# First two tiles of a fused attention and GELU kernel: 64x64 score products on plain transposed k, casts and loads in a new order

## The chip, the cores and the metric

The kernel runs on one core of a Trainium2 chip. The metric is the device time of one execution in microseconds, as a median over runs. A profile of one execution shows what each engine did: TensorE (PE, with its weight loads as PEld), VectorE (DVE), ScalarE (ACT), GpSimd (POOL), and SyncE (SP), whose queue issues the DMAs.

## The reference

```
q, k, v: (8, 8, 576, 64) fp32      w_in: (512, 2048)   w_out: (2048, 512)

for each batch b, head h and chunk of 64 rows (9 chunks of 576):
    scores = q_c @ k_c.T / 8
    attn   = exp(scores - max) / sum(exp(scores - max))
    out    = attn @ v_c
x = out as (8 * 576, 8 * 64) = (4608, 512)
h = x @ w_in
y = (0.5 * h * (1 + erf(h / sqrt 2))) @ w_out          # (4608, 512) fp32
```

Each chunk of 64 rows attends only to itself, so the attention is small: 64x64 scores for each of 576 pairs of head and chunk. The two dense products hold nearly all of the arithmetic.

## The kernel before

**Tiles.** The work is cut into nine tiles of 512 tokens: tile t < 8 holds eight chunks of batch t, the last tile the ninth chunk of all batches. Each tile goes through attention, which fills `x`, then through `mm1_slot` (16 slices f of 128 hidden columns, four matmuls of 128x512 each over ks, Gelu on ACT into `h`) and `mm2_slot` (four blocks of 128 tokens, 16 matmuls each). The attention of tile t+1 is put, by hand, between the matmuls of tile t. The order of instructions on every engine is the order in which the program writes them (`tc.manual_schedule`).

**Groups.** Two heads make a group g, four groups a tile. Of each group, q and k arrive in fp32 (`load_qk`), are cast to bf16 (`cast_qk`), transposed by TensorE into PSUM (`transposed`, four matmuls of 128x128) and copied back to SBUF: q into `qT` (`att_Tq`, L181), k into `k_bd` (`att_Tk`, L188). `k_bd` is block-diagonal: its off-diagonal blocks are zeroed once (`zero_k`), and the two heads are copied into the diagonal ones, so that one 128x128 product per chunk gives both heads' scores (`att_S`, L296, eight matmuls of 64 columns). ACT takes the exponential into `pT`.

**Sums.** The sum of the exponentials over keys runs along partitions. In tile 0, groups 0 and 1 use a product with `ones_bd` and two DVE transposes around a reciprocal (`att_sum`), groups 2 and 3 products with `ones_r` and back with `ident_f` (`att_sum_pe`, L348 and L357) and an ACT copy (L361). Tile 1 uses `att_sums` and `att_rc`. `att_av` multiplies with the block-diagonal `v_bd`, which `cast_v` (L169) fills, four quarter casts a group, and DVE scales the result into `x` (L372).

**Tiles 2 to 8** take another road: DMA transposes and 64x64 products on four quadrants of the array (`quad_S`, L227, and `quad_av`, L279). The change doesn't touch them.

**The opening.** All loads go through SP's queue, in program order, into six staging buffers used in turn: q and k of tile 0 in four parts each, v in eight, w_in in pieces of 512 columns, then w_out in four pieces (`load_w_out`) with q, k and v of tile 1 between them. Every piece is cast to bf16 by DVE, ACT or POOL as the program says. `keep_warm` issues matmuls on zeros whose result nobody reads.

**Tile 0's dense part.** `mm1_slices` computes the first two slices of h (L405), `phase` the rest (L415) and then the second product. For tile 0 that goes by rows of f (`mm2_rows`, L488, slots 0 to 11: every token block at once, so that w_out may arrive late), then by token blocks (L434, slots 12 to 15). The dictionary handed to `phase` says which parts of tile 1's attention stand ahead of which slot; `T`, `S_`, `U` and `A` are its lists of transposes, scores, sums and AV products. PSUM is shared out in three pools: `ps_mm` (three buffers), `ps_tp` (two, the transposes, and tile 1's later scores and AV), `ps_at` (three).

Of the kernel before, what the change touches and what calls it, by code (L numbers as in the profile page):

```python
# [11 lines left out]
def kernel(  # L12
# [9 lines left out]
    nc = tc.nc  # L22
# [45 lines left out]
    v_bds = [consts.tile([P, CT, G, P], bf16, name=f"v_bd{i}") for i in range(NV)]  # L68
    k_bds = [consts.tile([P, CT, P], bf16, name=f"k_bd{i}") for i in range(G)]

    def zero_v(i, eng):
        eng.memset(v_bds[i][0:CH, :, :, CH:P], 0.0)
        eng.memset(v_bds[i][CH:P, :, :, 0:CH], 0.0)

    def zero_k(k_bd, eng):
        eng.memset(k_bd[0:CH, :, CH:P], 0.0)
        eng.memset(k_bd[CH:P, :, 0:CH], 0.0)

# [98 lines left out]

    def att_Tq(t, g, copy):
        tp = transposed(t, "q", g)
        qT = work.tile([P, CT, CH], bf16, tag="qT", name="qT", bufs=5)  # L180
        copy(qT[:].rearrange("p i (c j) -> p i c j", j=J), tp)  # L181
        tiles[t]["qT", g] = qT

    def att_Tk(t, g, copy):
        tp = transposed(t, "k", g)
        for r in range(2):
            sl = slice(CH * r, CH * (r + 1))
            copy(k_bds[g][sl, :, sl].rearrange("p i (c j) -> p i c j", j=J), tp[sl])  # L188


# [100 lines left out]
    def att_S(t, g):  # L291
        st = tiles[t]
        pool, tag = (ps_tp, "tp") if t == 1 and g > 1 else (ps_at, "at")
        s_ps = pool.tile([P, CT, CH], f32, tag=tag, name="s_ps")
        for i in range(CT):
            nc.tensor.matmul(s_ps[:, i, :], k_bds[g][:, i, :], st["qT", g][:, i], start=True, stop=True)  # L296
        pT = work.tile([P, CT, CH], bf16, tag="pT", name="pT", bufs=5)
        nc.scalar.activation(pT[:], s_ps[:], Act.Exp, scale=scale)
        st["pT", g] = pT

    def att_sum(t, g, later=False):
        pT = tiles[t]["pT", g]
        sum_ps = ps_at.tile([P, MT], f32, tag="at", name="sum_ps")
        nc.tensor.matmul(sum_ps[:], ones_bd[:], pT[:], start=True, stop=True)
        t1 = work.tile([P, NB, 32], f32, tag="t1", name="t1", bufs=2)
        rc = work.tile([P, NB, 32], f32, tag="rc", name="rc", bufs=4)
        tiles[t]["rc", g] = rc
        nc.vector.transpose(t1[:], sum_ps[:].rearrange("p (n e) -> p n e", e=32))

        def rest_of_it():  # L310
            r1 = work.tile([P, NB], f32, tag="r1", name="r1", bufs=2)
            nc.vector.reciprocal(r1[:], t1[:, :, 0])
            nc.vector.transpose(rc[:], r1[:].to_broadcast([P, NB, 32]))
        if later:
            return rest_of_it
        rest_of_it()

# [46 lines left out]

    def att_av(t, g):
        st = tiles[t]
        pool, tag = (ps_tp, "tp") if t == 1 and g > 1 else (ps_at, "at")
        av_ps = pool.tile([P, CT, CH], f32, tag=tag, name="av_ps")
        for i in range(CT):
            nc.tensor.matmul(av_ps[:, i, :], v_bds[t % NV][:, i, g, :], st["pT", g][:, i, :], start=True, stop=True)  # L370
        x, av, rc = st["x"][:, g, :], av_ps[:].rearrange("p i e -> p (i e)"), st["rc", g][:]
        nc.vector.tensor_tensor(x, av, rc.rearrange("p n e -> p (n e)"), op=mybir.AluOpType.mult)  # L372

    NB = MT // 32
    DV, AC, PO = nc.vector.tensor_copy, nc.scalar.copy, nc.gpsimd.tensor_copy

    def att_units(t, cq=DV, ck=DV):
        tiles[t]["x"] = xpool.tile([P, G, MT], bf16, tag="x", name="x")
        T = []
        for g in range(G):  # L380
            T += [lambda g=g: att_Tq(t, g, cq), lambda g=g: att_Tk(t, g, ck if t == 0 or g % 2 == 0 else DV)]
        S_ = [lambda g=g: att_S(t, g) for g in range(G)]
        if t > 0:
            U = [lambda g=g: att_rc(t, g) for g in range(G)]
        else:
            U = [lambda g=g: att_sum(t, g) for g in range(G)]
        A = [lambda g=g: att_av(t, g) for g in range(G)]
        return T, S_, U, A


# [19 lines left out]
    def mm1_slot(t, f):  # L410
        if f == 0:
            tiles[t]["h"] = hpool.tile([P, FF, MT], bf16, tag="h", name="h")
        h_ps = ps_mm.tile([P, MT], f32, tag="mm", name="h_ps")
        for ks in range(KS):
            nc.tensor.matmul(h_ps[:], w_in_sb[:, ks, f * P:(f + 1) * P], tiles[t]["x"][:, ks, :],  # L415
                             start=(ks == 0), stop=(ks == KS - 1))
        nc.scalar.activation(tiles[t]["h"][:, f, :], h_ps[:], Act.Gelu)  # L417

    NQ = 4
# [92 lines left out]

    NWC = 4
    WC = d_ff // NWC
    FC = FF // NWC

# [9 lines left out]

    def load_w_out(c):
        raw = stage_tile()[:].rearrange("p (f n) -> p f n", f=FC)
        nc.sync.dma_start(raw, w_out_v[:, c * FC:(c + 1) * FC, :])

        def cast(i, copy):
            copy(w_out_sb[:, c * FC + i, :], raw[:, i, :])
        return cast

    def keep_warm(n):
        warm = ps_mm.tile([P, MT], f32, tag="mm", name="warm")
        for _ in range(n):
            nc.tensor.matmul(warm[:], rest[:, 0:P], rest[:], start=True, stop=True)

# [5 lines left out]
    with tc.manual_schedule():  # L545
# [5 lines left out]
        act_table(Act.Exp)  # L551
        keep_warm(7)
        zero_k(k_bds[0], nc.gpsimd)
        zero_k(k_bds[1], nc.gpsimd)
        zero_v(0, nc.vector)
        T, S_, U, A = att_units(0, DV, AC)
        cast_qk(0, "k", 0, PO)
        zero_k(k_bds[2], nc.gpsimd)
        cast_qk(0, "k", 1, PO)
        zero_k(k_bds[3], nc.gpsimd)  # L560
        cast_qk(0, "k", 2, PO)
        cast_qk(0, "k", 3, PO)
        for g in range(G - 1):
            for r in range(2):
                cast_v(0, g, r, (PO, PO))
        cast_v(0, G - 1, 0, (PO, PO))
        win[0](0, PO)
        cast_qk(0, "q", 0, DV)
        T[0]()
        cast_qk(0, "q", 1, DV)  # L570
        T[1]()
        keep_warm(3)
        T[2]()
        S_[0]()
        T[3]()
        cast_qk(0, "q", 2, DV)
        keep_warm(1)
        T[4]()
        keep_warm(1)
        S_[1]()  # L580
        cast_qk(0, "q", 3, DV)
        U[0]()
        T[5]()
        T[6]()
        T[7]()
        U[1]()
        S_[2]()
        keep_warm(1)
        S_[3]()
        keep_warm(1)  # L590
        act_table(Act.Gelu)
        p2 = att_sum_pe(0, 2)
        p3 = att_sum_pe(0, 3)
        A[0]()
        A[1]()
        p2()
        cast_v(0, G - 1, 1, (DV, DV))
        A[2]()
        win[0](1, AC)
        p3()  # L600
        A[3]()
        win.append(load_w_in(NWC - 1))
# [3 lines left out]
        load_qk(1, "q")  # L606
        wout.append(load_w_out(1))
        for c in range(1, NWC):
            for i in range(4):
                win[c](i, DV if i % 2 == 0 else PO)  # L610
            if c == 1:
                load_qk(1, "k")
            else:
                wout.append(load_w_out(c))
            if c < 3:
                r = slice(CH * (c - 1), CH * c)
                o = slice(CH * (2 - c), CH * (3 - c))
                nc.gpsimd.memset(v_bds[1][r, :, :, o], 0.0)
# [3 lines left out]
        for g in range(G):  # L622
            cast_qk(1, "q", g, DV if g == 0 else PO)
        for i in range(FC):
            wout[1](i, DV if i % 2 == 0 else PO)
        for g in range(G):
            cast_qk(1, "k", g, DV if g % 2 == 0 else PO)
        for i in range(FC):
            wout[2](i, PO)
# [5 lines left out]

        T, S_, U, A = att_units(1, AC, AC)
        def next_qk():
            for nm in "qk":
                load_qk(2, nm)
        over = []  # L640

        def sums():
            over.append(att_sums(1))
            over[0](1)
        mm, at = (ps_mm, "mm"), (ps_at, "at")
        mm1_slices(0, (mm, mm), (((0, 1), range(KS)),))
        phase(0, {0: [lambda: act_table(Act.Exp)],
                      2: [T[0]], 3: [T[2]], 4: [T[4], T[6]], 7: [T[1], T[3]], 8: [T[5], S_[0]],
                      9: [T[7], S_[1], next_qk], 10: [S_[2], lambda: att_sum(1, 0), lambda: wout[3](2, DV)],
                      11: [lambda: wout[3](3, AC), S_[3]], 12: [lambda: cast_v(1, 1, 0, (AC, AC)), lambda: cast_v(1, 1, 1, (AC, AC)), sums],  # L650
                      13: [A[0], lambda: over[0](2), lambda: over[0](3), U[1]], 14: [A[1], U[2]], 15: [A[2], U[3]]},
              by_rows=True, first=2)

        def last_av():
            A[3]()
            rows_out(0, 3)
# [90 lines left out]
```

## Time and profile before

| | |
|---|---|
| runs | 287.43, 287.48, 285.85 us; median 287.43 us |
| profiled execution | 286.87 us, of which 285.1 us from the first to the last instruction |
| busy | PE 275.7 us, ACT 174.3, DVE 113.5, POOL 84.2 |
| PE busy, 0 to 17.81 us | 13.73 of 17.81 us |
| PE busy, 17.81 to 33 us | 15.14 of 15.19 us |
| PE busy, 33 to 51 us (tile 1's attention among tile 0's second product) | 17.67 of 18.00 us |
| bytes moved, 17.81 to 33 us | 395 GB/s, the DMA engines' share 1.07 |

TensorE's matmuls are pipelined: a 512-column matmul is recorded with 379 ns, while the next one starts 216 ns behind it. So a busy PE says only that something is in flight; the distance between the starts tells how fast it goes. A few matmul records are missing, which shows as a distance of twice 216 ns. A bracket at the end of a line of the timeline gives the engine's idle time ahead of it and what ended it.

### The profile page before, as it was taken

Reading aid. Unit: us, or ns where it says so; the run is one execution under the profiler, and the core shown is the slowest. Engines: PE = TensorE matmul, PEld = TensorE weight load, DVE = VectorE, ACT = ScalarE, POOL = GpSimd, SP = SyncE. Lnnn points to the kernel's source line nnn. Section 1 sums busy time; section 2 is a strip of 40 time slices with the busy share of each in tenths; the row PEclk is TensorE's granted clock in tenths of the full one; section 3 lists DMA queues with packets and bytes.
Section 4 is the critical chain, followed back from the end, with each engine's and each line's share of the span. In section 5 each row is a group of like instructions: output and inputs, shape, how many; then the busy total and the mean of one; then the engine's idle time right before and its main releaser. Section 6 shows DMA issues by size and latency. Waiting matters only on the chain.

```text
span 285.1 us, 5771 instructions
## 1 busy us (share of the span) xinstructions
PE 275.7 (97%) x2288; PEld 134.2 (47%) x2317; DVE 113.5 (40%) x211; ACT 174.3 (61%) x357; POOL 84.2 (30%) x146
## 2 busy tenths in 40 slices
PE   7699999999999999999999999999999999999995
PEld 3464555445444454445444544454445444444444
DVE  6866358306800686047304630364026501600011
ACT  3867768876657776685577556755676467227400
POOL 7769767612561003504501700053002000000000
PEclk9999999999999999999999999999999999999999
DMA  7999999999999988999799449993942100210033
GB/s 228 245 363 402 393 356 268 226 267 250 278 217 250 239 200 236 268 203 283 226 201 261 131 129 212 160 231 106 175 100 78 74 2 0 76 74 0 2 74 74
DMA packets 119435, 53.86 MB, mean 189 GB/s; under 512 B 97776, under 2 KB 112368, under 8 KB 119408
## 3 DMA queue, kind: packets, MB, share of 16 engines
q1 hardware_dynamic: 119248, 53.36, 72.4%
q8 instruction: 18, 0.29, 0.4%
q10 hardware_dynamic: 160, 0.13, 0.2%
q14 instruction: 9, 0.07, 0.1%
HBM read 36.70 MB, written 9.44 MB: 162 GB/s over the span
## 4 chain that ended last, share of the span: by engine, by line
PE 92%; DMA 2%; POOL 2%; SPq 1%; issue 1%; ACT 0%; DVE 0%
PE h_ps L415 41%; PE y_ps L434 39%; PE y_ps L488 3%; PE h_ps L405 2%; DMA arrival<-in_k_dram 2%; PE s_ps L227 2%; POOL v_bd L169 2%; PE av_ps L279 2%; PE y_ps L466 1%; SPq L114 1%; PE tp L175 1%; PE av_ps L370 1%; ACT k_bd L188 0%; PE s_ps L296 0%; PE rc_ps L357 0%
## 5 line engine op out<-in xcount | busy, mean ns | idle before, releaser
L415 PE MATMUL h_ps<-x,w_in_sb 128*128 128x512 bf16 x539 | 119.3, 379 | 0.5
L434 PE MATMUL y_ps<-w_out_sb,h 128*128 128x512 bf16 x496 | 112.4, 379 | 1.1 <-issue 0.3
L417 ACT ACTIVATE h<-h_ps 128x512 bf16<-128x512 f32 x137 | 81.7, 598 | 51.0 <-PE h_ps L415 51.0
L415 PEld LDWEIGHTS <-w_in_sb 128*128 128x128 bf16 x548 | 53.6, 98 | 64.6
L434 PEld LDWEIGHTS <-h 128*128 128x128 bf16 x512 | 49.1, 98 | 57.9 <-issue 0.2
L164 POOL CAST q_nat<-arrival 128x512 bf16<-128x512 f32 x31 | 18.0, 624 | 82.0 <-DMA arrival<-in_q_dram 56.3
L261 DVE TENSOR_REDUCE total<-part 128x32 f32<-128x64 f32 x14 | 2.8, 197 | 71.2 <-ACT part L258 71.2
L449 DVE COPY y_sb<-y_ps 128x512 f32<-128x512 f32 x11 | 7.6, 690 | 47.2 <-PE y_ps L434 29.0
L200 POOL CAST v_nat<-arrival 128x1024 bf16<-128x1024 f32 x14 | 14.3, 1042 | 37.3 <-DMA arrival<-in_v_dram 37.3
L449 ACT COPY y_sb<-y_ps 128x512 f32<-128x512 f32 x24 | 13.8, 583 | 18.6 <-PE y_ps L434 15.1
L286 DVE TENSOR_TENSOR x<-av_ps,rc 128x512 bf16<-128x512 f32 x28 | 17.7, 688 | 12.0 <-PE av_ps L279 11.7
L543 ACT ACT_TABLE_LOAD x16 | 20.5, 1283 | 1.0 <-PEq L731 0.7
L248 DVE TENSOR_REDUCE part<-pt 128x16 f32<-128x512 bf16 x28 | 19.2, 686 | 1.0
L245 DVE STREAM_TRANSPOSE pt<-pT 128x256 f32<-128x256 f32 x28 | 12.2, 436 | 15.6 <-ACT pT L234 15.6
L162 POOL CAST k_nat<-arrival 128x512 bf16<-128x512 f32 x28 | 16.5, 616 | 2.4 <-DMA arrival<-in_k_dram 2.3
L234 ACT ACTIVATE pT<-s_ps 128x512 bf16<-128x512 f32 x28 | 14.4, 600 | 2.4 <-PE s_ps L227 2.4
L258 ACT COPY part<-part 32x32 f32<-32x32 f32 x56 | 12.2, 219 | 4.9 <-DVE part L248 4.2
L488 PE MATMUL y_ps<-w_out_sb,h 128*128 128x512 bf16 x46 | 11.6, 379 | 0.1
L169 POOL CAST v_bd<-arrival 64x256 bf16<-64x256 f32 x26 | 10.5, 404 | 1.4
L188 ACT COPY k_bd<-tp 64x512 bf16<-64x512 bf16 x12 | 6.9, 578 | 6.3 <-PE tp L175 6.2
L272 DVE STREAM_TRANSPOSE rc<-rb 128x512 f32<-128x512 f32 x14 | 9.7, 691 | 0.2
L272 DVE STREAM_TRANSPOSE rc<-across 128x512 f32<-128x512 f32 x14 | 9.3, 668 | 0.0
(80 smaller groups left out, 169.8 us busy)
## 6 DMA issues: line engine op xcount, KB each, us to landing
out_dram<-y_sb SPq DMA_DIRECT2D x32, 256.0 KB, 2.9
arrival<-in_v_dram SPq DMA_DIRECT2D x58, 128.0 KB, 3.1
arrival<-in_k_dram SPq DMA_DIRECT2D x28, 256.0 KB, 5.9
arrival<-in_q_dram SPq DMA_DIRECT2D x7, 1024.0 KB, 6.2
arrival<-in_moe_w_out_dram SPq DMA_DIRECT2D x4, 1024.0 KB, 12.2
arrival<-in_moe_w_in_dram SPq DMA_DIRECT2D x6, 512.0 KB, 7.0
arrival<-in_v_dram SPq DMA_DIRECT2D x28, 64.0 KB, 2.7
arrival<-in_q_dram SPq DMA_DIRECT2D x4, 256.0 KB, 3.9
```

Of the source, the lines that this page charges most:

```text
L162: copy(st[nm][:, :, g], st[nm + "f"][:, :, g].rearrange("p (q r) d -> p q r d", r=2))
L164: copy(st[nm][:, g].rearrange("p j r d -> p r j d"), st[nm + "f"][:, 2 * g:2 * g + 2])
L169: copy(v_bds[t % NV][to, c:CT:2, g, to], tiles[t]["vf"][CH * c:CH * (c + 1), 2 * g + r])
L248: nc.vector.tensor_reduce(st["part", g2][:, c, :, :, 0], pt[:].rearrange("p n e u -> p n u e"), axis=mybir.AxisListType.X, op=mybir.AluOpT ...
L272: nc.vector.transpose(rc[:], tiles[t]["rb", g2][c].to_broadcast([P, NB, 32]))
L286: nc.vector.tensor_tensor(x.rearrange("p n (e u) -> p n e u", u=2), st["av"][g2][c][:].rearrange("p n (e u) -> p n e u", u=2), st["rc", 2 ...
L415: nc.tensor.matmul(h_ps[:], w_in_sb[:, ks, f * P:(f + 1) * P], tiles[t]["x"][:, ks, :], start=(ks == 0), stop=(ks == KS - 1))
L417: nc.scalar.activation(tiles[t]["h"][:, f, :], h_ps[:], Act.Gelu)
L434: nc.tensor.matmul(y_ps[:], st["h"][:, f, ms * P:(ms + 1) * P], w_out_sb[:, f, :], start=(f == 0), stop=(f == FF - 1))
L449: (AC if ms < 3 and t + 1 < NT else DV)(y_sb[:], y_ps[:])
L488: nc.tensor.matmul(tiles[t]["y_ps", ms][:], tiles[t]["h"][:, fi, ms * P:(ms + 1) * P], w_out_sb[:, fi, :], start=(fi == 0), stop=False)
L543: nc.scalar.activation(act_scratch[:], rest[:, 0:1], func)
```

## The change

In tiles 0 and 1 k is transposed and copied like q, into one plain tile `kT` by a single full-width copy (`att_T` takes the place of `att_Tq` and `att_Tk`); `k_bd` and its zeroing go. The scores of a chunk are now two 64x64 products, one per head, at array positions (0, 0) and (64, 64).

In the opening, the order of instructions is written anew: 42 warming matmuls of 64 columns stand for 7 of 512, and one where there were three behind the first k; ACT casts V of group 2, POOL the other groups; the slices of w_in's first piece change hands; the Gelu table is loaded behind ACT's cast of w_in; the three steps of a sum (`t`, `r`, `rc`) and the scaling of x can be issued apart from each other.

The second piece of w_out is loaded in two parts, three rows of f ahead of tile 1's k and the fourth behind it; POOL casts the fourth behind its k casts. In tile 1, DVE copies k of the odd groups and ACT of the even ones, as before, but one copy each; the second q and k transposes and the scores stand in other slots.

```
-    def att_Tk(t, g, copy):
-        tp = transposed(t, "k", g)
-        for r in range(2):
-            sl = slice(CH * r, CH * (r + 1))
-            copy(k_bds[g][sl, :, sl].rearrange("p i (c j) -> p i c j", j=J), tp[sl])
+    def att_T(t, nm, g, copy):
+        tp = transposed(t, nm, g)
+        xT = work.tile([P, CT, CH], bf16, tag=nm + "T", name=nm + "T", bufs=5)
+        copy(xT[:].rearrange("p i (c j) -> p i c j", j=J), tp)
+        tiles[t][nm + "T", g] = xT
...
         for i in range(CT):
-            nc.tensor.matmul(s_ps[:, i, :], k_bds[g][:, i, :], st["qT", g][:, i], start=True, stop=True)
+            for r in range(2):
+                rs = slice(CH * r, CH * (r + 1))
+                nc.tensor.matmul(s_ps[rs, i, :], st["kT", g][rs, i], st["qT", g][rs, i], start=True, stop=True,
+                                 tile_position=(CH * r, CH * r))
...
-    def load_w_out(c):
+    def load_w_out(c, first=FC):
         raw = stage_tile()[:].rearrange("p (f n) -> p f n", f=FC)
-        nc.sync.dma_start(raw, w_out_v[:, c * FC:(c + 1) * FC, :])
+
+        def load(a, b):
+            nc.sync.dma_start(raw[:, a:b], w_out_v[:, c * FC + a:c * FC + b, :])
...
+        load(0, first)
+        cast.rest = lambda: load(first, FC)
         return cast
...
-    def keep_warm(n):
+    def keep_warm(n, cols=MT):
         warm = ps_mm.tile([P, MT], f32, tag="mm", name="warm")
         for _ in range(n):
-            nc.tensor.matmul(warm[:], rest[:, 0:P], rest[:], start=True, stop=True)
+            nc.tensor.matmul(warm[:, 0:cols], rest[:, 0:P], rest[:, 0:cols], start=True, stop=True)
```

The opening of the changed kernel, from the first warming matmuls to the first Gelu table (`t0`, `r0`, `rc0` and `t1`, `r1`, `rc1` are the three steps of the sums of groups 0 and 1; `x0` is the scaling of group 0):

```
        keep_warm(42, CH)
        zero_v(0, nc.vector)
        Tq, Tk, S_ = att_units(0, DV, (AC, AC))
        for g in range(G):
            cast_qk(0, "k", g, PO)
        for g in (0, 1, 3):
            for r in range(2):
                cast_v(0, g, r, (PO, PO))
        win[0](1, PO)
        cast_qk(0, "q", 0, DV); Tq[0](); cast_qk(0, "q", 1, DV); Tk[0]()
        keep_warm(1); S_[0](); keep_warm(1); Tq[1]()
        t0, r0, rc0 = att_sum(0, 0)
        cast_qk(0, "q", 2, DV); Tk[1](); Tq[2](); cast_qk(0, "q", 3, DV)
        S_[1](); Tk[2](); t0(); Tq[3](); r0()
        t1, r1, rc1 = att_sum(0, 1)
        S_[2](); Tk[3](); keep_warm(1); t1()
        p2 = att_sum_pe(0, 2)
        keep_warm(1); S_[3](); rc0()
        x0 = att_av(0, 0, later=True)
        p3 = att_sum_pe(0, 3)
        r1(); rc1(); x0()
        cast_v(0, 2, 0, (AC, AC)); p2(); cast_v(0, 2, 1, (AC, AC)); p3()
        att_av(0, 1)
        win[0](0, AC)
        act_table(Act.Gelu)
        att_av(0, 2); att_av(0, 3)
```

Behind it, the loads and tile 1:

```
-        wout.append(load_w_out(1))
+        wout.append(load_w_out(1, 3))
...
             if c == 1:
                 load_qk(1, "k")
+                wout[1].rest()
...
-        for i in range(FC):
+        for i in range(3):
             wout[1](i, DV if i % 2 == 0 else PO)
         for g in range(G):
             cast_qk(1, "k", g, DV if g % 2 == 0 else PO)
+        wout[1](3, PO)
...
-                      2: [T[0]], 3: [T[2]], 4: [T[4], T[6]], 7: [T[1], T[3]], 8: [T[5], S_[0]],
-                      9: [T[7], S_[1], next_qk], 10: [S_[2], lambda: att_sum(1, 0), lambda: wout[3](2, DV)],
-                      11: [lambda: wout[3](3, AC), S_[3]], 12: [lambda: cast_v(1, 1, 0, (AC, AC)), lambda: cast_v(1, 1, 1, (AC, AC)), sums],
+                  2: [Tq[0]], 3: [Tq[1]], 4: [Tq[2], Tq[3]], 7: [Tk[0], Tk[1]],
+                  8: [Tk[2], S_[0], Tk[3], S_[1], S_[2], next_qk], 9: [S_[3], first_sum],
+                  10: [lambda: wout[3](2, DV)], 11: [sums, lambda: wout[3](3, AC)], 12: [casts_and_spreads],
```

More of the change, by code (lines that the diff above doesn't have):

```diff
@@ L68 @@
     v_bds = [consts.tile([P, CT, G, P], bf16, name=f"v_bd{i}") for i in range(NV)]
-    k_bds = [consts.tile([P, CT, P], bf16, name=f"k_bd{i}") for i in range(G)]
     def zero_v(i, eng):
@@ L73, in zero_v @@
         eng.memset(v_bds[i][CH:P, :, :, 0:CH], 0.0)
-    def zero_k(k_bd, eng):
-        eng.memset(k_bd[0:CH, :, CH:P], 0.0)
-        eng.memset(k_bd[CH:P, :, 0:CH], 0.0)
     w_in_sb = consts.tile([P, KS, d_ff], bf16, name="w_in_sb")
@@ L176, in transposed @@
         return tp[:, 0].rearrange("p j (i c) -> p i c j", i=CT)
[L178 to L182, printed above, removed]
-    def att_Tk(t, g, copy):
-        tp = transposed(t, "k", g)
-        for r in range(2):
-            sl = slice(CH * r, CH * (r + 1))
-            copy(k_bds[g][sl, :, sl].rearrange("p i (c j) -> p i c j", j=J), tp[sl])
+    def att_T(t, nm, g, copy):
[3 more added lines that the diff above has]
+        tiles[t][nm + "T", g] = xT
     def flip(t, nm):
@@ L299, in att_S, with att_sum @@
         st["pT", g] = pT
-    def att_sum(t, g, later=False):
-        pT = tiles[t]["pT", g]
+    def att_sum(t, g):
         sum_ps = ps_at.tile([P, MT], f32, tag="at", name="sum_ps")
-        nc.tensor.matmul(sum_ps[:], ones_bd[:], pT[:], start=True, stop=True)
+        nc.tensor.matmul(sum_ps[:], ones_bd[:], tiles[t]["pT", g][:], start=True, stop=True)
         t1 = work.tile([P, NB, 32], f32, tag="t1", name="t1", bufs=2)
+        r1 = work.tile([P, NB], f32, tag="r1", name="r1", bufs=2)
         rc = work.tile([P, NB, 32], f32, tag="rc", name="rc", bufs=4)
         tiles[t]["rc", g] = rc
[L308 to L316, printed above, removed]
+        return (lambda: nc.vector.transpose(t1[:], sum_ps[:].rearrange("p (n e) -> p n e", e=32)),
+                lambda: nc.vector.reciprocal(r1[:], t1[:, :, 0]),
+                lambda: nc.vector.transpose(rc[:], r1[:].to_broadcast([P, NB, 32])))
     def att_sums(t):
@@ L363, in att_sum_pe, with att_av @@
         return spread
-    def att_av(t, g):
+    def att_av(t, g, later=False):
         st = tiles[t]
@@ L370, in att_av, with scaled, att_units @@
             nc.tensor.matmul(av_ps[:, i, :], v_bds[t % NV][:, i, g, :], st["pT", g][:, i, :], start=True, stop=True)
-        x, av, rc = st["x"][:, g, :], av_ps[:].rearrange("p i e -> p (i e)"), st["rc", g][:]
-        nc.vector.tensor_tensor(x, av, rc.rearrange("p n e -> p (n e)"), op=mybir.AluOpType.mult)
+        def scaled():
+            x, av, rc = st["x"][:, g, :], av_ps[:].rearrange("p i e -> p (i e)"), st["rc", g][:]
+            nc.vector.tensor_tensor(x, av, rc.rearrange("p n e -> p (n e)"), op=mybir.AluOpType.mult)
+        if later:
+            return scaled
+        scaled()
     NB = MT // 32
     DV, AC, PO = nc.vector.tensor_copy, nc.scalar.copy, nc.gpsimd.tensor_copy
-    def att_units(t, cq=DV, ck=DV):
+    def att_units(t, cq, cks):
         tiles[t]["x"] = xpool.tile([P, G, MT], bf16, tag="x", name="x")
[L379 to L388, printed above, removed]
+        Tq = [lambda g=g: att_T(t, "q", g, cq) for g in range(G)]
+        Tk = [lambda g=g: att_T(t, "k", g, cks[g % 2]) for g in range(G)]
+        return Tq, Tk, [lambda g=g: att_S(t, g) for g in range(G)]
     def mm1_slices(t, pools, steps):
@@ L417, in mm1_slot @@
         nc.scalar.activation(tiles[t]["h"][:, f, :], h_ps[:], Act.Gelu)
+    NWC = 4
+    WC = d_ff // NWC
+    FC = FF // NWC
     NQ = 4
@@ L511, in pool_cast_qk @@
                 cast_qk(t, nm, g, PO)
-    NWC = 4
-    WC = d_ff // NWC
-    FC = FF // NWC
     def load_w_in(c, parts=1):
@@ L551 @@
         act_table(Act.Exp)
-        keep_warm(7)
-        zero_k(k_bds[0], nc.gpsimd)
-        zero_k(k_bds[1], nc.gpsimd)
+        keep_warm(42, CH)
         zero_v(0, nc.vector)
[L556 to L563, printed above, removed]
+        Tq, Tk, S_ = att_units(0, DV, (AC, AC))
+        for g in range(G):
+            cast_qk(0, "k", g, PO)
+        for g in (0, 1, 3):
             for r in range(2):
                 cast_v(0, g, r, (PO, PO))
-        cast_v(0, G - 1, 0, (PO, PO))
-        win[0](0, PO)
+        win[0](1, PO)
         cast_qk(0, "q", 0, DV)
-        T[0]()
+        Tq[0]()
         cast_qk(0, "q", 1, DV)
-        T[1]()
-        keep_warm(3)
-        T[2]()
+        Tk[0]()
+        keep_warm(1)
         S_[0]()
-        T[3]()
+        keep_warm(1)
+        Tq[1]()
+        t0, r0, rc0 = att_sum(0, 0)
         cast_qk(0, "q", 2, DV)
-        keep_warm(1)
[L578 to L587, printed above, removed]
+        Tk[1]()
+        Tq[2]()
+        cast_qk(0, "q", 3, DV)
+        S_[1]()
+        Tk[2]()
+        t0()
+        Tq[3]()
+        r0()
+        t1, r1, rc1 = att_sum(0, 1)
+        S_[2]()
+        Tk[3]()
+        keep_warm(1)
+        t1()
+        p2 = att_sum_pe(0, 2)
         keep_warm(1)
         S_[3]()
-        keep_warm(1)
-        act_table(Act.Gelu)
[L592 to L601, printed above, removed]
+        rc0()
+        x0 = att_av(0, 0, later=True)
+        p3 = att_sum_pe(0, 3)
+        r1()
+        rc1()
+        x0()
+        cast_v(0, 2, 0, (AC, AC))
+        p2()
+        cast_v(0, 2, 1, (AC, AC))
+        p3()
+        att_av(0, 1)
+        win[0](0, AC)
+        act_table(Act.Gelu)
+        att_av(0, 2)
+        att_av(0, 3)
         win.append(load_w_in(NWC - 1))
@@ L634 @@
                 cast_v(1, g, r, (PO, PO))
-        T, S_, U, A = att_units(1, AC, AC)
+        Tq, Tk, S_ = att_units(1, AC, (AC, DV))
         def next_qk():
@@ L640, with first_sum, casts_and_spreads, av @@
         over = []
+        def first_sum():
+            for op in att_sum(1, 0):
+                op()
         def sums():
             over.append(att_sums(1))
+        def casts_and_spreads():
+            for r in range(2):
+                cast_v(1, 1, r, (AC, AC))
             over[0](1)
+        def av(g):
+            return lambda: att_av(1, g)
+        def spread(g):
+            return lambda: att_rc(1, g)
         mm, at = (ps_mm, "mm"), (ps_at, "at")
@@ L647 @@
         phase(0, {0: [lambda: act_table(Act.Exp)],
-                      2: [T[0]], 3: [T[2]], 4: [T[4], T[6]], 7: [T[1], T[3]], 8: [T[5], S_[0]],
-                      9: [T[7], S_[1], next_qk], 10: [S_[2], lambda: att_sum(1, 0), lambda: wout[3](2, DV)],
-                      11: [lambda: wout[3](3, AC), S_[3]], 12: [lambda: cast_v(1, 1, 0, (AC, AC)), lambda: cast_v(1, 1, 1, (AC, AC)), sums],
-                      13: [A[0], lambda: over[0](2), lambda: over[0](3), U[1]], 14: [A[1], U[2]], 15: [A[2], U[3]]},
+                  2: [Tq[0]], 3: [Tq[1]], 4: [Tq[2], Tq[3]], 7: [Tk[0], Tk[1]],
+                  8: [Tk[2], S_[0], Tk[3], S_[1], S_[2], next_qk], 9: [S_[3], first_sum],
+                  10: [lambda: wout[3](2, DV)], 11: [sums, lambda: wout[3](3, AC)], 12: [casts_and_spreads],
+                  13: [av(0), lambda: over[0](2), lambda: over[0](3), spread(1)], 14: [av(1), spread(2)],
+                  15: [av(2), spread(3)]},
               by_rows=True, first=2)
         def last_av():
-            A[3]()
+            att_av(1, 3)
             rows_out(0, 3)
```

## The prediction

> **What bounds the kernel now.** I read the page first (busy shares and the chain that ended last), then the chain of waits in order of time, then TensorE's own timeline around the two places that the change touches, and the other engines' timelines over the first 20 us.
>
> ```profile
> span 285.1 us, 5771 instructions
> ...
> PE 275.7 (97%) x2288; PEld 134.2 (47%) x2317; DVE 113.5 (40%) x211; ACT 174.3 (61%) x357; POOL 84.2 (30%) x146
> ...
> PE 92%; DMA 2%; POOL 2%; SPq 1%; issue 1%; ACT 0%; DVE 0%
> ```
>
> TensorE carries 92% of the chain; everything else on it lies before 17.8 us. The timeline of TensorE shows where the dense part begins:
>
> ```profile
> 16.30 1.09 PE L357 MATMUL rc_ps<-ident_f,rr 128*64 128x128 f32 x16
> ...
> 17.33 0.41 PE L370 MATMUL av_ps<-pT,v_bd 128*128 128x64 bf16 x8
> 17.81 1.67 PE L405 MATMUL h_ps<-x,w_in_sb 128*128 128x512 bf16 x7
> ```
>
> From 17.81 us on 512-column matmuls start every 0.216 us (L415, 42 of them in 9.06 us), and apart from the stalls named below nothing interrupts them. So two numbers decide: when the first h_ps starts, and how much TensorE time tile 1's attention costs between 33 and 51 us, where its slots stand between matmuls of tile 0. A microsecond in either place moves the end by a microsecond.
>
> Before 17.8 us the order is by latency. K of the last group lands at 9.85 us, POOL casts it to 10.58 us, then casts V back to back (twelve casts to 15.95 us, 0.46 us apart), and AV of group 2 waits for the twelfth.
>
> **Part 1, the scores as 64x64 products.** Before, one group is 8 matmuls of 128x128 weights, 0.029 us apart (0.23 us). The same 64x64 shape stands in the trace at L227, in the later tiles:
>
> ```profile
> 63.03 0.81 PE L415 MATMUL h_ps<-x,w_in_sb 128*128 128x512 bf16 x3
> 63.77 0.80 PE L227 MATMUL s_ps<-q_t,k_t 64*64 64x64 bf16 x64
> 64.50 0.39 PE L434 MATMUL y_ps<-w_out_sb,h 128*128 128x512 bf16 x1
> ```
>
> The last L415 starts at 63.46 us, so at 0.216 us apart its follower was due at 63.67; the first L227 starts at 63.77. That is 0.09 us for going in. L227 issues four quadrants 0.003 us apart and repeats every 0.032 us, with 0.02 us more in the first round. Its last matmul starts at 64.38, the next was due 0.03 us later, and y_ps starts at 64.50: 0.09 us for coming out. One visit costs 0.09 + 0.02 + 0.09 = 0.20 us beside its rounds.
>
> The changed kernel uses two quadrants (rows 0 to 63 into outputs 0 to 63, and the other half), 8 rounds a group. If a round lasts as long as at L227, a group is 8 x 0.032 = 0.256 us against 0.233. Bounds of a round: 0.027 us (64 columns at the rate at which 512 take 0.216) and 0.064 (the two halves one after the other). I take 0.032, since L227 has the same tile shape and writes both halves of one bank in the same round.
>
> In tile 1 the new order is Tk2, S0, Tk3, S1, S2, one y_ps row of f, S3: three visits. 3 x 0.20 + 4 x 0.023 = **+0.69 us** (+0.5 to +1.7 over the bounds of a round).
>
> [...]
>
> **Part 2, one copy of k.** Before, each k goes out of PSUM in two half copies. In tile 1 they make the third transpose wait for its buffer:
>
> ```profile
> 38.34 0.61 PE L175 MATMUL tp<-ident,k_nat 128*128 128x128 bf16 x8
> 38.79 1.03 PE L488 MATMUL y_ps<-w_out_sb,h 128*128 128x512 bf16 x4
> 39.99 0.38 PE L175 MATMUL tp<-ident,k_nat 128*128 128x128 bf16 x4 [0.17 <-ACT k_bd L188]
> ```
>
> The fourth y_ps of the second row starts at 39.44 and a follower was due at 39.66, so TensorE loses 0.34 us (the page's 0.17 counts from the modelled end). The two half copies end at 39.95 (38.77 + 0.58 + 0.59 us). One full-width copy takes what ACT's L181 copies take, 0.58 us, so the buffer is free at 39.35, before the transpose is due: **-0.34 us**. What is late next is S2: it starts 1.29 us behind its own transpose (0.22 transpose, 0.48 visit of S0, 0.22 transpose, 0.37 entry and rounds of S1), and transpose complete (0.39) plus ACT copy (0.61) take 1.00. That leaves 0.3 us; past it S2 costs what ACT is late. Bound 0 to +0.3. DVE's copies for the odd groups (0.69 instead of 1.39) have 0.7 us to spare.
>
> **Part 3, the order of the loads.** k of tile 1 lands before the last quarter of w_out's second piece, 256 KB sooner; at the 400 GB/s of this stretch that is 0.65 us. Nothing waits: the first k transposes were not held by k (38.34, directly behind y_ps). The moved quarter (row f=7) lands when k landed before, 37.0 us; POOL casts it after two k casts of 0.81 us from about 36.4, so done near 38.7 against a need at 38.8. SP gets one DMA issue more, about 1 us, in a queue that runs ahead of the data (this piece was issued at 21.3 and landed at 34.2). Cost 0, cover 0.1 us; if that is gone, up to +0.5. Row f=8, cast at 40.2 and used at 40.44 before, is used 0.5 us later in the new order, so its slack grows.
>
> **Part 4, the first 18 us.** Removed: eight zeroings of k_bd on POOL (0.52 each), which also stood beside DVE's casts; those take 0.72 to 0.78 beside POOL and 0.42 alone (9.70 us). Added on ACT before the first h_ps: four V casts (0.40 each), with its one w_in cast (0.62) now standing last; moved behind that: the Gelu table load (1.28 + 0.20). I walk the new order with those durations, two values where POOL decides how long DVE's casts take.
>
> kT0 is copied by 6.63 (6.05 + 0.58), S0 issues at 6.69, exp0 runs 7.17 to 7.77 (7.72 to 8.32 before). But Tq1 now stands behind S0 and a warming matmul: 7.27 against 6.84. DVE then goes in a row: qT1 to 8.38, cast q2 to 8.75/9.05, transposes, qT2 to 9.9/10.2, cast q3 to 10.3/10.9, t0 (0.72) to 11.0/11.6, qT3 to 11.7/12.3. On ACT: exp1 to 10.2/10.5, kT2 to 10.8/11.1, exp2 to 12.0/12.6, kT3 to 12.6/13.2, exp3 to 13.7/14.3 (13.82 before). TensorE: sT of group 3, then rc_ps of group 2 (1.09) to 15.05/15.65. From there **ACT** sets the end: rc copy 0.59, two V casts 0.84, rc copy 0.59, the w_in cast 0.62, each right behind the other: 17.7/18.3. DVE ends x of group 3 at 18.35/18.95, needed six matmuls (1.29 us) after the first h_ps, so not the limit. The first half of w_in landed before 16.3. The table load ends 1.5 us behind the cast; the first Gelu isn't due until 1.9 us behind it.
>
> So the first h_ps stands at 17.77 to 18.37 against 17.81: **+0.26 us** in the middle. That is the removed work eaten by a longer ACT chain, not a gain.
>
> **Sum.** +0.69 - 0.34 + 0 + 0.26 = +0.61 us. The profiled execution took 286.87 us (285.1 span, 1.8 around it): 287.5. The median of the three runs, 287.43, lies 0.56 above it, so the same sum on the median gives 288.0. I take **287.7**.
>
> **Rivals.** *The clock comes up late (slower).* Matmuls of 512 columns last 0.634 us at first and 0.379 later; transposes in fours fall from 0.60 (5.41 us) to 0.39 (6.84 us):
>
> ```profile
> L538 PE MATMUL warm<-rest x13: 379/634/634, 1.2 to 13.0; 128*128 128x512 bf16 x13
> ```
>
> TensorE was then busy from 1.2 us with only short gaps. The new opening has 42 matmuls of 64 columns; at half rate (0.055 each) they end near 3.5 us instead of 4.2, and behind them stand one warming matmul where there were three, and gaps up to 1 us. [...] For it: fewer columns (42 x 64 and 4 x 512 against 14 x 512). Against: at half rate everything lasts twice as long, so the gaps close.
>
> [...]
>
> *The opening is shorter than I walk (faster).* If ACT's chain starts from the better values and S0's 0.55 us survives, h_ps starts at 17.1, where x of group 3 (17.7 less 1.29, with 0.6 gained) allows it. -0.7 there, +0.35 in tile 1: 286.5. w_out's f=8 leaves room for about 0.7 of that.
>
> *The halves do not run at the same time.* Round 0.064: 4 x 0.256 more in tile 1 and 0.25 in each S of the opening: 289.2.
>
> *The change buys no single copy* (S2 takes over the stall of the transpose): +0.3, 288.0.
>
> **How the numbers follow.** Forecast 0.44 (286.9 to 288.4); clock late but up before 17.8, 0.14 (288.3); clock late past it, 0.12 (291); faster opening 0.16 (286.5); halves in series 0.08 (289.2); S2's stall 0.06 (288.0). A measurement of this kernel tells about 1% from no change, which is 2.9 us. Over that on the slow side lie the late clock and a little of the halves with other losses: 0.17. On the fast side at most 0.34 + 0.9 can be gained (w_in lands at 16.2 and needs a cast), so 0.04 for what I have missed; within 1%, 0.79. The range 285.9 to 290.4 leaves out most of the clock case and the far end of the gain.
>
> **What would show it.** L296's successor should have 64 matmuls in tile 1, in rounds of 0.032 us, with 0.09 us before and behind each visit; no wait of a transpose for a k copy near 39 us; first L405 between 17.7 and 18.4 with a w_in cast of ACT ending right before it; transposes of four at 0.39 from the second q on. It is wrong if h_ps starts before 17.2, if the matmuls behind it are 0.43 us apart, or if a wait for f=7 or S2 of over 0.3 us stands between 38 and 42 us.

## The result, and the profile after

The changed kernel takes 288.75 us (median of 17 runs) against 287.16 us for the kernel before (17 runs): a ratio of 1.0052, with a 95% interval of 1.0027 to 1.0077. It is slower by some 1.5 us (0.8 to 2.2), inside the predicted range and within 1%, and 1 us above the forecast of 287.7 us. The profiled execution took 288.32 us against 286.87 before.

The page of the changed kernel, its span, busy shares and the chain that ended last:

```profile
span 286.2 us, 5972 instructions
...
PE 278.1 (97%) x2413; PEld 136.3 (48%) x2413; DVE 108.6 (38%) x207; ACT 172.4 (60%) x355; POOL 79.0 (28%) x136
...
PE 94%; ACT 2%; DMA 1%; DVE 1%; issue 0%; POOL 0%; SPq 0%; POOLq 0%
```

POOL's 2% in the old chain (the V casts) are gone, and ACT has taken their place. DVE and POOL work 5 us less each; the time is none the better for it. Two places carry the difference.

**The opening.** ACT's timeline of the changed kernel, 14 to 19 us:

```profile
14.18 0.81 ACT L164 CAST v_bd<-arrival 64x256 bf16<-64x256 f32 x2
15.66 0.58 ACT L347 COPY rc<-rc_ps 128x512 f32<-128x512 f32 x1 [0.67 <-PE rc_ps L343]
16.27 0.83 ACT L164 CAST v_bd<-arrival 64x256 bf16<-64x256 f32 x2
17.12 0.58 ACT L347 COPY rc<-rc_ps 128x512 f32<-128x512 f32 x1
17.73 0.62 ACT L508 CAST w_in_sb<-arrival 128x512 bf16<-128x512 f32 x1
```

From 15.66 us one instruction stands right behind the other, and TensorE waits for the last of them:

```profile
18.40 1.90 PE L388 MATMUL h_ps<-x,w_in_sb 128*128 128x512 bf16 x8 [0.64 <-ACT w_in_sb L508]
```

Here all eight matmuls of the first two slices are recorded. Of the kernel before only seven were, from 17.81 us. Its weight loads (PEld) show that the missing one is the first:

```profile
17.58 0.98 PEld L405 LDWEIGHTS <-w_in_sb 128*128 128x128 bf16 x6
```

Counted by weight loads the opening therefore ends at 18.40 us against 17.58, **+0.82 us**. What makes it late shows in TensorE's timeline. First two rows of the kernel before, then the changed kernel between 7 and 10.5 us:

```profile
5.41 0.60 PE L175 MATMUL tp<-ident,k_nat 128*128 128x128 bf16 x4 [0.34 <-POOL k_nat L164]
...
6.84 0.39 PE L175 MATMUL tp<-ident,q_nat 128*128 128x128 bf16 x4
```

```profile
7.25 0.64 PE L170 MATMUL tp<-ident,q_nat 128*128 128x128 bf16 x4
...
9.00 0.61 PE L170 MATMUL tp<-ident,q_nat 128*128 128x128 bf16 x4 [0.27 <-DVE q_nat L159]
...
9.97 0.40 PE L170 MATMUL tp<-ident,k_nat 128*128 128x128 bf16 x4
```

In the changed kernel four transposes last 0.6 us until 9.7 us and 0.4 behind it; in the kernel before this happened at 6.6 us. At half rate a 128-column transpose starts 0.107 us behind the last, at the full rate 0.056 us. The array ran at half rate some 3.15 us longer.

**Tile 1.** TensorE's timeline from the first k transposes on:

```profile
39.16 0.61 PE L170 MATMUL tp<-ident,k_nat 128*128 128x128 bf16 x8
39.61 1.03 PE L475 MATMUL y_ps<-w_out_sb,h 128*128 128x512 bf16 x4
40.47 0.39 PE L170 MATMUL tp<-ident,k_nat 128*128 128x128 bf16 x4
40.79 0.44 PE L286 MATMUL s_ps<-qT,kT 64*64 64x64 bf16 x16
41.16 0.40 PE L170 MATMUL tp<-ident,k_nat 128*128 128x128 bf16 x4
41.49 0.69 PE L286 MATMUL s_ps<-qT,kT 64*64 64x64 bf16 x32
42.11 1.04 PE L475 MATMUL y_ps<-w_out_sb,h 128*128 128x512 bf16 x4
43.08 0.44 PE L286 MATMUL s_ps<-qT,kT 64*64 64x64 bf16 x16
```

The third transpose, at 40.47, no longer waits. S0 should have followed its transposes at 40.70 and starts at 40.79; the three visits (stretches of 64x64 products among 128-wide ones) at 40.79, 41.49 and 43.08 lose 0.093 us going in and 0.096 coming out each. The stretch from tile 1's first k transpose to its first h_ps (both by weight loads) lasts 11.69 us against 11.28: **+0.41 us**. From there to the end nothing differs by over 0.1 us. This is one trace against one: a second trace of the kernel before, read below, has 11.73 us in this stretch, because of another wait.

### The profile page after: what moved, and what is told of

Same layout as the page of the kernel before. It is cut to its first block, busy times and chain, and to the rows that moved or that the text cites. A ratio compares the mean times of both kernels' runs of the same rounds, so it can differ in the third digit from the quotient of the medians.

```text
span 286.2 us, 5972 instructions
## 1 busy us (share of the span) xinstructions
PE 278.1 (97%) x2413; PEld 136.3 (48%) x2413; DVE 108.6 (38%) x207; ACT 172.4 (60%) x355; POOL 79.0 (28%) x136
## 4 chain that ended last, share of the span: by engine, by line
PE 94%; ACT 2%; DMA 1%; DVE 1%; issue 0%; POOL 0%; SPq 0%; POOLq 0%
PE h_ps L398 41%; PE y_ps L421 39%; PE y_ps L475 4%; PE h_ps L388 2%; PE av_ps L267 2%; PE s_ps L215 2%; PE tp L170 1%; PE y_ps L453 1%; DMA arrival<-in_k_dram 1%; PE s_ps L286 1%; DVE qT L176 0%; ACT pT L289 0%; ACT rc L347 0%; PE rc_ps L343 0%; DVE q_nat L159 0%; PE av_ps L356 0%
## 5 line engine op out<-in xcount | busy, mean ns | idle before, releaser
L421 PE MATMUL y_ps<-w_out_sb,h 128*128 128x512 bf16 x512 | 113.7, 380 | 0.0
L188 POOL CAST v_nat<-arrival 128x1024 bf16<-128x1024 f32 x14 | 14.3, 1040 | 37.6 <-DMA arrival<-in_v_dram 37.6
L274 DVE TENSOR_TENSOR x<-av_ps,rc 128x512 bf16<-128x512 f32 x28 | 17.7, 687 | 12.1 <-PE av_ps L267 11.8
L475 PE MATMUL y_ps<-w_out_sb,h 128*128 128x512 bf16 x48 | 11.7, 380 | 0.0
L164 POOL CAST v_bd<-arrival 64x256 bf16<-64x256 f32 x24 | 9.8, 407 | 1.3
L256 ACT COPY across<-rb 64x16 f32<-64x16 f32 x28 | 5.7, 202 | 3.8 <-DVE rb L251 3.5
```

What stands on the lines that cost most here:

```text
L274: nc.vector.tensor_tensor(x.rearrange("p n (e u) -> p n e u", u=2), st["av"][g2][c][:].rearrange("p n (e u) -> p n e u", u=2), st["rc", 2 ...
L421: nc.tensor.matmul(y_ps[:], st["h"][:, f, ms * P:(ms + 1) * P], w_out_sb[:, f, :], start=(f == 0), stop=(f == FF - 1))
L475: nc.tensor.matmul(tiles[t]["y_ps", ms][:], tiles[t]["h"][:, fi, ms * P:(ms + 1) * P], w_out_sb[:, fi, :], start=(fi == 0), stop=False)
```

## What sets the rate: the table behind the experiments

The trace records the granted clock of the array with its times; the variants named below are described in the next section. In all fourteen traces the full rate lasts a whole number of 3.413 us from its start to its end near the kernel's end (82 in the kernel before: 279.89 us; 81 after: 276.48), so both changes lie on one grid of 3.413 us. Its phase is not tied to the kernel's start: two traces of the kernel before have the change at 6.58 and 5.61 us. For each stretch of that grid I added up how long the array streams, that is, takes in columns: the columns of each matmul at half rate (512 columns 0.427 us), a 64x64 one counted half, since two run at once (0.003 us apart in the changed kernel's S0). This share is my reckoning from the starts, not a figure that the trace gives.

| trace | doubles at (us) | streaming share of the stretch before | largest share of an earlier stretch | weights of first h_ps (us) | tile 1, first k transpose to h_ps (us) |
|---|---|---|---|---|---|
| before | 6.58 | 0.77 | 0.58 | 17.58 | 11.28 |
| before, again | 5.61 | 0.91 | 0.30 | 17.52 | 11.73 |
| changed | 9.73 | 0.79 | 0.54 | 18.40 | 11.69 |
| changed, again | 13.36 | 0.80 | 0.71 | 19.15 | 11.69 |
| old warming in the changed | 10.46 | 0.79 | 0.72 | 18.85 | 11.69 |
| old casts in the changed | 9.86 | 0.76 | 0.54 | 17.88 | 11.88 |
| one visit | 19.38 | near full (fp32 products in a row) | 0.75 | 20.68 | 11.34 |
| wide scores | 8.49 | 0.84 | 0.66 | 18.29 | 11.11 |
| new warming in the old kernel | 11.22 | 0.94 | 0.75 | 17.65 | 11.46 |
| filled opening | 3.87 | 0.78 | 0 | 17.53 | 11.84 |
| filled, one visit | 7.20 | 0.89 | 0.76 | 17.41 | 11.91 |
| split halves in the old kernel | 5.25 | 0.87 | 0.20 | 17.70 | 11.46 |
| filled, one visit, ACT's cast | 5.69 | 0.94 | 0.32 | 17.17 | 11.35 |
| the same, w_out's piece whole | 5.34 | 0.95 | 0.22 | 18.33 | 11.34 |

In these fourteen traces the rate doubles at the end of the first stretch whose share reaches about 0.76; no stretch of 0.75 or less did it, and 0.76 did once (old casts) and once not (filled, one visit), so the line is known to 0.01 at best. With gaps in most openings, the change came between 3.87 and 19.38 us from the start of the span, where the first matmul stands at 1.2.

## The experiments

**Old warming.** Edit, in the changed kernel:

```
-        keep_warm(42, CH)
+        keep_warm(7)
...
-        keep_warm(1)
+        keep_warm(2)            # behind the first k's transposes
```

> The changed kernel with 7 warming matmuls of 512 columns at the start again and two behind the first k. Theory: the new warming is why transposes in fours last 0.61 us until 9 us; with the old one they last 0.39 from the second q on (near 7 us), the sT products of group 3 start 0.3 to 0.5 us sooner than 14.34, and the first h_ps comes at 17.9 to 18.1 instead of 18.40. Rival: ACT's row of casts sets the start whatever the clock does: h_ps stays within 0.15 us of 18.40. Against the kernel before: +0.3% by the theory, +0.45% by the rival.

Measured: 288.54 us, ratio 1.0046 (1.0024 to 1.0068). The rate doubled at 10.46 us, later than in the changed kernel, and h_ps came at 18.85. The theory as put was wrong: more warming alone did not bring it forward in this trace. The first k landed at 4.87 us here, so TensorE stood 0.87 us ahead of its transposes, and the stretch to 7.04 us reached 0.65. That led to the table.

**Old casts.** Edit, in the changed kernel: POOL casts V of groups 0 to 2, half of 3 and the first slice of w_in; DVE the rest of V, ACT the second slice.

```
-        cast_v(0, 2, 0, (AC, AC)); p2(); cast_v(0, 2, 1, (AC, AC)); p3()
-        att_av(0, 1); win[0](0, AC)
+        cast_v(0, 3, 1, (DV, DV)); p2(); p3()
+        att_av(0, 1); win[0](1, AC)
```

> The changed kernel with V and the first piece of w_in shared out as before: POOL casts V of groups 0 to 2 and half of 3, then the first slice of w_in; DVE the other half of group 3, ACT only the second slice of w_in between the two rc copies. Warming as in the changed kernel. Theory: ACT's row (rc, two V casts, rc, w_in cast) ends last before the first h_ps; without it h_ps starts at 17.6 to 17.8 and the time falls by 0.6 to 0.8 us against the changed kernel. Rival: the late clock alone costs the opening, the casts are covered: 18.3 to 18.4, no change.

Measured: 288.9 us, ratio 1.0052 (1.0029 to 1.0074). The weights of h_ps come at 17.88, near the forecast, and nothing is won. DVE's timeline shows the next in the row:

```profile
16.50 1.06 DVE L164 CAST v_bd<-arrival 64x256 bf16<-64x256 f32 x2
17.60 1.89 DVE L360 TENSOR_TENSOR x<-av_ps,rc 128x512 bf16<-128x512 f32 x3
19.93 0.43 DVE L508 CAST w_in_sb<-arrival 128x512 bf16<-128x512 f32 x1 [0.44 <-DMA arrival<-in_moe_w_in_dram]
```

Three x end at 19.49, so h_ps stops among its own matmuls (0.33 us by the starts). The second half of w_in's piece landed at 19.9, where the changed kernel had it at 18.2, and costs 0.44 us more; why it landed later was not traced. The 0.52 us won at the first h_ps is lost again in these two waits.

**One visit.** Edit: slot 8 holds `Tk[2], Tk[3], S_[0], S_[1], S_[2], S_[3]`, slot 9 only `first_sum`.

> The changed kernel with tile 1's four groups of scores in one row, directly behind the fourth k transpose (all in slot 8). Theory: each change between 128-wide and 64x64 products costs TensorE 0.09 us, so two visits fewer give 0.36 us, less up to 0.15 for waiting on the k copies: tile 1's stretch from its first k transpose to its first h_ps is 0.2 to 0.4 us shorter than 11.69 us. Rival: the pairs themselves cost the time, not the going in and out: unchanged within 0.05.

Measured: 288.27 us, ratio 1.0041 (1.0015 to 1.0067). Tile 1's stretch is 11.34 us, 0.35 shorter, as the theory has it and not its rival: the going in and out is the cost. TensorE's timeline has the four groups in one row of 64:

```profile
43.91 0.61 PE L170 MATMUL tp<-ident,k_nat 128*128 128x128 bf16 x8
44.45 1.29 PE L286 MATMUL s_ps<-qT,kT 64*64 64x64 bf16 x64
45.67 0.60 PE L475 MATMUL y_ps<-w_out_sb,h 128*128 128x512 bf16 x2
```

The opening of this trace is that of the changed kernel, and there the rate did not double before 19.38 us:

```profile
15.68 3.68 PE L343 MATMUL rc_ps<-ident_f,rr 128*64 128x128 f32 x32
...
20.69 0.60 PE L388 MATMUL h_ps<-x,w_in_sb 128*128 128x512 bf16 x2 [0.50 <-ACT w_in_sb L508]
```

The two rc_ps rows took 3.68 us where the changed kernel's trace has 1.97, and this execution took 291.32 us. That is the rival "the clock comes up late", past 17.8 us, priced at 291. One of the 17 executions of the changed kernel took 292.05 us; it has no trace, so that it is the same case is not shown.

**Wide scores.** Edit: tile 1's scores as eight products with 128 columns of k as weights.

```
+            if t == 1:
+                wide = st["kT", g][:].rearrange("p i c -> p (i c)")[:, CH * min(i, CT - 2):CH * min(i, CT - 2) + P]
+                nc.tensor.matmul(s_ps[:, i, :], wide, st["qT", g][:, i], start=True, stop=True)
+                continue
```

> The changed kernel with tile 1's scores taken with 128 columns of the plain k as weights, eight products a group (which mixes heads and chunks: tile 1's scores are left wrong, the time alone counts). Everything else as changed. Theory: without visits of 64x64 the stretch from tile 1's first k transpose to its first h_ps falls from 11.69 us by 0.6 to 0.7, to below the 11.3 of the kernel before, because the wait of the third k transpose is gone too. Rival: the single copy or the new slots cost something of their own: it falls by less than 0.4.

Measured: tile 1's stretch 11.11 us, 0.58 shorter than changed and 0.17 shorter than before, as the theory has it, less 0.15 us in which S2 now waits for its k copy. The median stays at 288.73 (ratio 1.0047, 1.0028 to 1.0067), so it shows none of this, although the profiled execution took 287.6.

**New warming in the old kernel.** Edit, in the kernel before: 42 of 64 columns for 7 of 512, one for three.

> The kernel before with the changed kernel's warming alone: 42 matmuls of 64 columns for 7 of 512, one for three behind the first k. Theory from the six traces so far: TensorE's rate doubles only at the end of a stretch of 3.413 us, on a grid of its own, in which matmuls stream at least 0.76 of the time (0.76 to 0.84 just before each doubling, 0.75 and less in all others). With the new warming the stretch to 6.6 us fails, and the rate doubles near 10 us or later. The old opening waits for POOL's V casts (to 15.95), so that costs little: weights of the first h_ps at 17.6 to 18.0 while the doubling is before 14 us, 19 or later if it comes behind that; +0.1% to +0.3% in the median. Rival: warming has no part in it: doubling before 7 us, h_ps at 17.6, no change.

Measured: 287.61 us, ratio 1.0011 (0.9992 to 1.003). The rate doubled at 11.22 us, and the first h_ps moved by 0.07 us. TensorE's timeline:

```profile
16.08 0.41 PE L370 MATMUL av_ps<-pT,v_bd 128*128 128x64 bf16 x8
16.41 1.09 PE L357 MATMUL rc_ps<-ident_f,rr 128*64 128x128 f32 x16
```

AV still stands behind POOL's V casts near 16 us. The late rate is covered there; in the changed order, which took V of one group off POOL, it isn't. The new warming alone cost little in the old order. That it costs more in the new one is read from these traces; the new order with an early rate and nothing else altered was not run.

**Filled opening.** Edit, in the changed kernel:

```
-        keep_warm(42, CH)
+        keep_warm(52, CH)
...
         Tq[0]()
+        keep_warm(9, CH)
         cast_qk(0, "q", 1, DV)
         Tk[0]()
-        keep_warm(1)
+        keep_warm(15, CH)
         S_[0]()
-        keep_warm(1)
         Tq[1]()
+        keep_warm(5, CH)
...
         Tk[1]()
+        keep_warm(9, CH)
```

> The changed kernel with warming matmuls of 64 columns in every gap of the first 9 us (52 at the start, 9 behind the first q transposes, 15 behind the first k's, 5 behind the second q's, 9 behind the second k's), so that TensorE streams without a break from 1.2 us. Theory: any stretch of the grid that lies within 1.2 to 9 us now passes 0.76, so the rate doubles between 4.6 and 8.0 us whatever the phase; first h_ps at 17.9 to 18.2 (18.40 in the changed kernel), no run of 291 us and more; median 0.4 to 0.8 us under the changed kernel's. Rival: the doubling depends on something else (time since the start, what the matmuls are): it comes at 8.5 us or later again, median unchanged.

Measured: 287.96 us, ratio 1.0034 (1.0014 to 1.0054), none of 12 runs above 290.3. The median is 0.8 us under the changed kernel's, but the intervals of the two ratios overlap, so the medians alone don't tell the two apart. The rate doubled at 3.87 us and h_ps came at 17.53, both earlier than I expected. ACT's timeline shows what the late rate had hidden:

```profile
14.98 0.83 ACT L164 CAST v_bd<-arrival 64x256 bf16<-64x256 f32 x2
15.83 0.59 ACT L347 COPY rc<-rc_ps 128x512 f32<-128x512 f32 x1
16.86 0.62 ACT L508 CAST w_in_sb<-arrival 128x512 bf16<-128x512 f32 x1 [0.44 <-DMA arrival<-in_moe_w_in_dram]
```

ACT's row now ends at 16.42, 1.3 us sooner than in the changed kernel, and then waits for w_in to land. So with the gaps filled the new order is the shorter one up to there, and its gain ends at a transfer.

Not all of the 1.3 us is the rate. The edit also takes away the warming matmul of 512 columns that stood right ahead of the second q's transposes; they start at 6.73 instead of 7.25. And DVE's cast of the fourth q took 0.42 us (9.29) instead of 0.74 (10.26), which is 0.3 us. The shorter transposes of the second and third q (0.40 instead of 0.61 to 0.64) give 0.45 us. How the 0.5 us at 6.73 divides between the rate and the missing matmul was not run apart.

**Filled opening, one visit.** Both edits.

> The filled opening and tile 1's scores in one visit. If the two parts are independent: 0.35 us less in tile 1 than the filled opening alone (stretch of 11.3 to 11.4 us from the first k transpose to the first h_ps of tile 1), and the median 0.9 to 1.1 us under the changed kernel's, so within 0.2% of the kernel before. If the visits' gain is given back later, the time is that of the filled opening.

Measured: 287.85 us, ratio 1.002 (1.0002 to 1.0038). The stretch of tile 1 is 11.91 us, not the 11.3 to 11.4 expected, since TensorE's timeline has a new wait:

```profile
39.19 1.02 PE L475 MATMUL y_ps<-w_out_sb,h 128*128 128x512 bf16 x4 [0.40 <-POOL w_out_sb L518]
```

This is row f=7, which the split load puts behind k and POOL casts behind two k casts. By the starts TensorE stands 0.57 us. The cover of 0.1 us is gone once the opening ends earlier: the wait was 0.15 us in the filled opening alone and 0 in the changed kernel.

**Split halves in the old kernel.** Edit, in `att_Tk`: `half = (AC, DV)[r] if t == 1 else copy`.

> The kernel before, in which tile 1's two half copies of a k go to ACT and DVE at once, where one engine made both. Theory: the third k transpose waits for its PSUM buffer only 0.7 us instead of 1.2, so TensorE's stop of 0.34 us near 39.4 is gone: stretch from tile 1's first k transpose to its first h_ps 10.9 to 11.0 us instead of 11.28, median -0.1%. Rival: the scores behind it wait for the copies in its place: 11.2 to 11.3.

Measured: 287.11 us, ratio 0.9992 (0.9971 to 1.0014), stretch 11.46: no gain, though not for the rival's reason. DVE's half of a k does not run beside ACT's half, it waits for it:

```profile
39.67 1.30 DVE L189 COPY k_bd<-tp 64x512 bf16<-64x512 bf16 x2 [0.84 <-ACT k_bd L189]
```

The transposes are done near 39.03, ACT's first half runs from 39.06 to 39.64, and DVE starts at 39.67. The only semaphore that DVE's copy waits for is one that ACT's copy raises, so this order was set in the program's waits; whether the two could read the tile at once was not seen.

**Filled, one visit, f=7 cast by ACT.** Edit: `wout[1](3, AC)` at the head of slot 7 in place of POOL's cast.

> The filled opening, one visit, and the late row of w_out (f=7) cast by ACT ahead of tile 1's first k transpose, where POOL did it behind its k casts. In the trace of the filled opening with one visit TensorE stood 0.57 us for that cast. Theory: with ACT, idle there, that wait goes; stretch from tile 1's first k transpose to tile 2's first 64x64 product near 25.7 us (26.26 there, 25.63 in the kernel before), median 0.4 to 0.6 us lower than 287.85, so level with the kernel before. Rival: the row has not landed by then either, and the wait stays above 0.3 us.

Measured: the wait is gone, the stretch is 11.35 us (25.70 to tile 2's first 64x64 product), the profiled execution took 286.98 us. The median, 287.81 (ratio 1.0026, 1.0007 to 1.0045), did not fall. A miss: the trace is level with the kernel before, the median isn't.

**Two second traces.**

> The kernel before once more, for a second trace of its opening. Theory of the grid: the rate doubles at the end of the first stretch that streams at least 0.76 of the time; with the old warming that is by 8.3 us at the latest in most phases. Weights of the first h_ps at 17.5 to 17.8, tile 1's third k transpose waits 0.3 us again.

> The changed kernel once more. Theory of the grid: doubling between 8 and 11 us, or behind 14 us, by the phase; first h_ps at 18.2 to 18.9 in the first case, 20 or later in the second. Rival (a fixed delay): 9.7 and 18.4 again.

Measured: 287.65 us for the kernel before, doubling at 5.61, h_ps at 17.52; its third transpose waited only 0.09 us, but k landed at 38.1, over 1 us later than first, and TensorE then stood 0.65 us for w_out's f=8. The changed kernel took 289.28 us: doubling at 13.36, h_ps at 19.15. So there is no fixed delay, but neither figure lies in the ranges expected (8 to 11 us or behind 14; 18.2 to 18.9 or 20 and later): the stretch to 9.94 us reached only 0.71. The rule of the table held, its forecast of when did not.

**w_out's piece whole again.** Edit, in the kernel with the filled opening, one visit and ACT's cast:

```
-        wout.append(load_w_out(1, 3))
+        wout.append(load_w_out(1))
...
-                wout[1].rest()
```

> The filled opening with one visit and ACT's cast of f=7, and the second piece of w_out loaded whole again, tile 1's k behind it. What the split is worth: k lands 0.65 us later (37.4 to 38.1), so the first k transposes wait 0 to 0.5 us; f=7 lands 0.65 sooner and waits for nothing. If the split is a cost of the changed kernel that the traces don't show (half a microsecond is left in the medians), the median falls to 287.2 to 287.4; if it is worth what its order promises, the median rises by 0.2 to 0.5 from 287.81; if it is neither, within 0.2.

Measured: 287.49 us, ratio 1.0013 (0.999 to 1.0036), not told apart from the kernel before, nor from 1.0026 with the split. The median fits none of the three cases of the forecast. In its trace the last k of tile 0 landed at 10.86 us, in the other thirteen at 9.45 to 10.05, and h_ps came at 18.33 with the rate up at 5.34: here a late landing stands beside an opening as late as with a late rate.

## Why the prediction came out as it did

The direction, the change of under 1% and the range were right. The sum was +0.61 us; the medians differ by 1.59 us and the traces by 1.16 us of span (0.82 in the opening, 0.41 in tile 1, -0.07 behind it). Tile 1's sum of +0.35 us came from the right mechanism. The opening was late for a reason that the forecast had set aside, and that the total stayed in the range is owed to its width, which had been drawn for that rival.

- **Going in and out of 64x64** (0.20 a visit, +0.69): right. 0.19 us by the starts, three visits, shown in tile 1's stretch by one visit (-0.35) and by wide scores (-0.58).
- **Pairs in rounds of 0.032 us**: right, S0's eight pairs start from 40.79 to 41.03, the two of a pair 0.003 us apart. The halves run at the same time; that rival is out.
- **The third transpose's wait** (-0.34): right against the trace it was read from; it is gone, and S2 did not take it over in the changed kernel. In the second trace of the kernel before the wait was only 0.09 us, so 0.34 is not its worth in every execution.
- **The split load** (0, cover 0.1, up to +0.5 without it): right in the changed kernel, and 0.57 where the opening was shortened.
- **The opening** (+0.26): the term that was mis-sized, measured +0.82. Its zero was 0.2 us late, because a missing record hid the first h_ps. Its walk took the rate as doubled at 6.6 us, where the changed kernel's came at 9.7. The forecast's own case failed here, and the rival of the late clock came in its milder form (priced at 288.3). The first h_ps at 18.40 meets the sign that was named for the forecast (17.7 to 18.4, ACT's w_in cast right before it), but that is luck: the walk had the late end from casts slowed beside POOL, and of those two only one was slow (0.74 us, the other 0.42). With the rate up early the row was also shorter than walked: exp3 ended at 13.0 in the filled opening, not at 13.7 to 14.3. Part of that is the warming matmul that this opening lacks. And with the rate late (9.86 us) but V and w_in shared out as before, the first h_ps came at 17.88: ACT's longer row and the late rate make it late together.
- **"Gaps close at half rate"**, held against the late clock: half right. In the changed kernel and its variants without filled gaps they closed to shares of 0.54 to 0.75 ahead of the stretch that doubled the rate, and that stretch had 0.76 or more. The late clock's prices, 288.3 and 291, rest on a guess of mine at how much later the rate doubles, which no run shows as a fixed delay: against 6.58 us in the first trace of the kernel before it came 3.15 us later in the changed kernel (288.32 us), 6.78 later in its second trace (289.28) and 12.80 later in one visit (291.32).

What stays open: with both causes mended in the trace, the median was 0.5 us above the kernel before, and wide scores' median kept nothing of 0.58 us. Single executions of one kernel spread over 2 to 4.6 us, and each variant has one trace, the two main kernels two. The last k of tile 0 lands up to 1.4 us apart in the traces, which would be enough; it wasn't shown that this makes the half microsecond. With w_out's piece whole again the ratio was 1.0013, which is not told apart from either side.

## What to carry to other kernels

Before shortening an opening, look at what the old order covered: the array's slow start cost 0.07 us while POOL's casts were last; in the new order, filling its gaps and dropping one warming matmul moved the first h_ps by 0.87 us. Count the visits to another shape of the array, not the matmuls in them, and put all of a kind in one visit: here going into and out of 64x64 cost 0.19 us a visit, and one visit in place of three took 0.35 us off tile 1. And a record missing at the head of a group moves the point that one counts from (17.81 us here, 17.58 by the weight loads): compare matmuls with their weight loads.

## What the runs showed of the hardware that I had not expected

- In all fourteen traces the rate of the array changed on a grid of 3.413 us, at the end of the first stretch that streamed about 0.76 of the time or more. The changed kernel and its variants whose gaps were not filled had earlier stretches of 0.54 to 0.75 and doubled anywhere from 8.5 to 19.4 us; with the gaps filled the rate doubled from 3.9 to 7.2 us.
- Transposes count towards that share. The stretch that doubled the rate in the kernel before held 0.25 of them in its 0.77. Without them it would have 0.52, less than the 0.76 of a stretch with no transposes that did not double it (filled, one visit).
- In the changed kernel two 64x64 products on opposite quarters of the array started 0.003 us apart, and a pair followed the last after 0.032 us; going into a row of them cost 0.093 us and coming out 0.096.
